# Moving shuffles, weight issues, sums, banks and late products in the first pair of an attention + MLP kernel

## The chip, the cores and the metric

The kernel runs on one core of one Trainium2 chip. The metric is device time in microseconds; lower is better. A profiled execution gives the trace that is quoted here. Engines are named as the profile names them: PE (TensorE), PEld (its weight loads), DVE (VectorE), ACT (ScalarE), POOL (GpSimd), SP (SyncE). A name such as L752 is line 752 of the kernel.

## The reference

Grouped-query attention (8 batches, 16 query heads, 4 key heads, 384 tokens, head size 64), followed by a residual MLP block over 1024 channels with a hidden width of 4096:

```
attn = softmax(q k^T / 8);  x = attn v          (8, 384, 1024)
a1  = alpha1 * x + beta1
tok = w_tok @ a1                                (mixes the 384 tokens)
u   = x + lam * tok
a2  = alpha2 * u + beta2
ch  = relu(a2 @ w_ch1) @ w_ch2                  (1024 -> 4096 -> 1024)
out = u + lam * ch
```

## The kernel before

**Stages.** The eight batches go in four pairs. An opening stage makes attention, token mixing and the turned a2 of batches 0 and 1 (`A` and `C` in the code). Then each pair runs a first product (a2 by w_ch1) and a second product (hidden by w_ch2); beside the second product of one pair, the attention of the next pair's two batches runs in small steps (`side`). Both products are done with seven block products in place of eight (a Strassen-like scheme), so there are sums and differences of operands, of weights and of results. The products are numbered 1 to 7; in the second product of the first pair the results of 2, 6, 7 and 4 are multiplied by lam and added to `out` by an accumulating DMA.

**Order.** The order of every engine's instructions is written by hand (`manual_schedule`): each engine runs its own instructions in the order of the code, and waits only for data, buffers and banks. In the opening stage a table `at` names for each of 36 turns (a quarter of a head pair's scores) what is emitted behind that turn's scores; a list behind it names the rest. In the products, a `yield` ends each segment of four matmuls (second product) and the table `plan` (`put(pair, phase, segment, ...)`) names what is emitted behind that segment.

**Names that the change touches.**

- `load_block(kind, gp)` (L553) issues from POOL the load of a quarter of the first product's weights, 512 KB in bf16, cast from float32; L1, L2, R1 and R2 are its four blocks, `gp` the pair of groups. With `home(c)` it goes to the arena, else to one of the six slots of the ring `w1`.
- `to_all(i, half, place)` (L1037) copies a row of 512 values to all partitions with a DVE shuffle; `to_all(2, ...)` makes alpha2, which `tok` needs (L334, on POOL in the opening stage).
- `tok(p)`: token mixing of a head pair on PE (L324, L328), its addition on DVE (L331), its product with alpha2 (L334). `turn(p)` turns the result on PE (L398), copied by ACT (L400); `C`'s first four are turned by DMA instead (L337). `av(p)`: probabilities by v on PE (L295), reciprocal and division on DVE (L300, L303). `a1(p)`: its product with g1 on DVE (L318, or L309 beside a second product).
- `diff_first(0, 4)` (L458) subtracts the turned a2 of both batches on DVE, an operand of product 7; `sums_first` (L454) makes another one.
- `share_banks(...)` opens the PSUM pools after the first product. `acc` has two banks for the accumulators of the second product, `sc0` to `sc2` two each for the attention. Ahead of it, Y (with product 4's sums, read by L702) had the banks 0 and 1, and X (read by L697) the banks 2 and 3.
- `second_product` has 21 turns of four segments: (product, third of the tokens) in the order 1, 2, 5 mixed, then 3, 6, 7 and 4, three each. Behind a turn ACT copies the bank (L764), and for products 6 and 7 DVE adds (L767); the result then stands in `later`. `flush(1)` takes one out of it twice a turn and emits `scaled`: the product with lam on POOL (L790) and the accumulating store from POOL (L442).
- `sum_w2`, `keep_w2`, `last_w2(c)`: differences of w_ch2 blocks on DVE (L499), stored by SP (L494); `last_w2` makes those of product 4 and frees a slot, and a free slot lets the queue issue its next load, here `load_w1` (L183, on POOL) for the next pair. `sum_w1` (L510, L515) makes sums of those for the next first product (L831; copied by L836).

The places of results are slices of one buffer; the next pair's first copies (L836) use the same buffer from s5 on:

```python
s2, s1, s5, s3 = ([snaps[:, (NST * i + ms) * 512:(NST * i + ms + 1) * 512] for ms in range(NST)] for i in range(4))
```

Of the kernel before, what the change touches and what calls it, by code (L numbers as in the profile page):

```python
# [13 lines left out]
def kernel(  # L14
# [27 lines left out]
    ADD = mybir.AluOpType.add  # L42
# [685 lines left out]
    def second_product(acc, later, flush, scaled):  # L728
# [17 lines left out]
        for k, (o, ms) in enumerate(turns):  # L746
            if (o, ms) not in xs_:
                begin(o, ms)
            x = xs_[o, ms]
            for t in range(NH):  # L750
                slot, rhs = raw[names[o], t // 4]
                nc.tensor.matmul(out=x, lhsT=lead_hid[:, t, FIRST2[o], ms * P:(ms + 1) * P],  # L752
                                 rhs=rhs[:, t % 4 * 512:(t % 4 + 1) * 512], start=(o in (1, 5) and t == 0), stop=(t == NH - 1),
                                 skip_group_check=True)
                if t % 4 == 3 and ms == NST - 1 and (o in (2, 3) or o == 4 and slot < RING):
                    free(slot)
                if t % 4 == 3 and t < NH - 1:
                    if t == 7 and turns[k + 1:] and turns[k + 1][0] in (3, 6, 7, 4):
                        begin(*turns[k + 1])
                    if t % 8 == 3 and later and later[0][1] != 4:  # L760
                        flush(1)
                    yield 1
            to = {1: s1, 2: s2, 5: s5, 3: s3, 6: s1, 7: s1, 4: s3}[o][ms]
            nc.scalar.copy(out=to, in_=x)  # L764
            if o in (6, 7):
                to = (s3 if o == 6 else s5)[ms]
                tt(out=to, in0=x, in1=to, op=ADD)  # L767
            if o in (2, 6, 7, 4):
                later.append((scaled, 1 if o == 2 else o, int(o in (7, 4)), ms, int(o in (6, 7)), to))
            yield 1  # L770

    def pair(i):
# [38 lines left out]

        if lead:
            yield from first_product(flush)
            share_banks("acc", "sc0", "sc1", "sc2")
            yield from second_product(pairs["acc"], later, flush, scaled)
            return

# [129 lines left out]
    with tc.manual_schedule(engines=order):  # L947
# [112 lines left out]
        scale_rows(1, nc.gpsimd)  # L1060
        split(1, 2, None, nc.gpsimd)
        load_v(1)
        for kind, gp in (("L1", 3), ("L2", 3), ("R1", 3), ("R2", 3), ("L1", 2), ("L2", 2)):
            load_block(kind, gp)

        def spill_all(b):
            nc.sync.dma_start(out=by_tok(out[b]), in_=xs[b])
# [30 lines left out]
        for c in range(4):  # L1098
            put(0, 0, (50, 72, 74, 44)[c], load_w2, "11", c)
            put(0, 0, (6, 14, 42, 46)[c], cast_w2, "21", c)  # L1100
            put(0, 1, (41, 43, 45, 47)[c], keep_w2, 1, c)
            put(0, 1, 38 + 2 * c, keep_w2, 3, c)
            put(0, 1, (9, 10, 13, 15)[c], sum_w2, 5, c)
            put(0, 1, (20, 21, 25, 26)[c], sums_first_hid, 2, c)
            put(0, 1, (28, 30, 31, 34)[c], sums_first_hid, 4, c)
            put(0, 1, (37, 40, 41, 43)[c], sum_w2, 6, c)
            put(0, 1, (44, 45, 49, 50)[c], sums_first_hid, 3, c)
            put(0, 1, (51, 54, 57, 58)[c], sum_w2, 7, c)
            put(0, 1, (60, 62, 64, 66)[c], last_w2, c)
# [29 lines left out]
        def product(n=1):  # L1139
            for _ in range(n):  # L1140
# [7 lines left out]
        A.q_transpose(1, 1, "tp")  # L1148
        at = {0: [(warmup, 3), (scale_rows, 0), (split, 0, 1, 0)], 1: [(A.k_transpose, 1, 1)],
              2: [(A.q_transpose, 2, 2, "av"), (split, 0, 1, 1)], 3: [(warmup, 1)],  # L1150
              4: [(A.av, 0)], 5: [(A.spread, lower, "tp"), (A.a1, 0)], 6: [(A.av, 1), (A.k_transpose, 2, 2, "tp"), (to_all, 2, 0, 0)],
              7: [(A.q_transpose, 4, 2, "av"), (A.a1, 1)], 8: [(A.av, 2), (to_all, 2, 1, 1), (flip_k, 1)],
              9: [(A.wtok_transpose, 0, "av"), (A.wtok_transpose, 1, "tp"), (flip_q, 1, 0, 4)],
              10: [(A.wtok_transpose, 2, "av"), (A.q_transpose, 6, 2, "mm"), (fill_h, 0)], 11: [(A.av, 3), (A.rows_r, "tp")],
              12: [(A.spread, upper, "av", "ACT"), (A.a1, 2), (fill_h, 4), (flip_q, 1, 4, 4)],
              13: [(A.tok, 0), (A.av, 4), (A.a1, 3)],
              14: [(A.tok, 1), (A.a1, 4)], 15: [(A.av, 5), (A.tok, 2), (A.a1, 5), (A.turn, 0, "tp")], 16: [(A.tok, 3), (A.turn, 1, "av")],
              17: [(A.av, 6), (A.a1, 6), (A.turn, 2, "tp")],
              18: [(A.tok, 4), (A.turn, 3, "av")], 19: [(A.av, 7), (A.a1, 7)], 20: [(A.tok, 5), (A.turn, 4, "tp")], 21: [(A.tok, 6)],
# [12 lines left out]
        for f, *a in ((C.turn, 4, "sc"), (C.av, 7), (early1, 10), (C.a1, 7), (early1, 11), (C.tok, 6), (C.turn, 5, "sc"), (early2, 10),  # L1172
                      (C.tok, 7), (early2, 11), (sums_first, 0, 2), (C.turn, 6, "sc"), (product, 2), (sums_first, 2, 1),
                      (C.turn, 7, "sc"), (sums_first, 3, 1), (spill_all, 1)):
            f(*a)
# [38 lines left out]
```

## Time and profile before

| | |
|---|---|
| median of 3 runs | 735.61 us (735.04 to 736.73) |
| profiled execution | 734.31 us |
| its span | 732.5 us |
| PE busy | 714.0 us (97%) |
| DVE busy | 542.6 us (74%) |
| ACT busy | 373.4 us (51%) |
| POOL busy | 200.6 us (27%) |
| granted TensorE clock | 1.00 |

The opening stage takes the first 60 us, the first pair's first product lasts until 130 us, its second product until 236 us. Rows of the profile's answers stand below. A row of the timeline has start, length (us), engine, line, operation, out<-in, shapes, count, and in brackets how long the engine stood idle before it and what ended that. A row of the waits has who waited for whom, the sum in us, how many times, the longest. A row of the DMA view has out<-in, the issuing queue, count, KB each and the us from issue to landing.

### The profile page before, as it was taken

What the parts mean: (1) busy time and instruction counts of PE and PEld (TensorE: products, weight loads), DVE (VectorE), ACT (ScalarE), POOL (GpSimd) and SP (SyncE); (2) the same over time, 40 slices, a digit from 0 to 9 for tenths busy, and PEclk for the clock granted to TensorE, in tenths of its full rate; (3) what the DMA queues carried; (4) which work ended last, traced back from release to release, by engine and by line L of the source; (5) the groups of instructions that cost most, each with busy time, mean ns of one, the idle gap of its engine ahead of it and who ended that gap; (6) DMA issues with size and microseconds to landing.
All of it is one profiled execution on the core that took longest, in us unless ns stands there. A gap on an engine that the chain in (4) does not pass through costs nothing.

```text
span 732.5 us, 14451 instructions
## 1 busy us (share of the span) xinstructions
PE 714.0 (97%) x5657; PEld 408.5 (56%) x5716; DVE 542.6 (74%) x1009; ACT 373.4 (51%) x566; POOL 200.6 (27%) x242
## 2 busy tenths in 40 slices
PE   8998999999999999999999999999999999999998
PEld 4665555455545566555555566655555566654444
DVE  8788876577897798649778988748958988762354
ACT  7877766545554666653433366663343366650000
POOL 8844243231073552201022344100002222000011
PEclk9999999999999999999999999999999999999999
DMA  9999999999999999979989999998999999937965
GB/s 166 184 236 205 192 188 225 228 250 211 366 309 251 182 184 200 208 232 218 261 193 205 179 162 195 210 221 211 276 227 178 212 126 145 169 123 261 304 173 102
DMA packets 197616, 153.26 MB, mean 209 GB/s; under 512 B 90540, under 2 KB 175892, under 8 KB 197292
## 3 DMA queue, kind: packets, MB, share of 16 engines
q0 software_dynamic: 109872, 64.47, 65.3%
q1 hardware_dynamic: 86988, 87.42, 43.4%
q8 instruction: 44, 0.72, 0.4%
q10 hardware_dynamic: 688, 0.46, 0.2%
q14 instruction: 24, 0.20, 0.1%
HBM read 155.23 MB, written 39.85 MB: 266 GB/s over the span
## 4 chain that ended last, share of the span: by engine, by line
PE 82%; DVE 9%; issue 3%; POOL 2%; DMA 2%; ACT 1%; DVEq 0%; POOLq 0%; ACTq 0%
PE C L897 28%; PE X L831 17%; PE Y L831 8%; PE C L752 6%; PE Z L831 4%; PE sc L260 4%; PE X L681 4%; PE sc L295 3%; PE Y L681 3%; PE sc L324 3%; DMA ops<-obuf 1%; DMA w<-in_moe_w_ch_dram 1%; DVE pad L565 1%; PE tok L324 1%; POOL w L553 1%
## 5 line engine op out<-in xcount | busy, mean ns | idle before, releaser
L897 PE MATMUL C<-w,arena 128*128 128x512 bf16 (+2 forms) x711 | 163.7, 373 | 1.6 <-issue 0.3
L269 ACT ACTIVATE es<-sc 128x1024 bf16<-128x1024 f32 x108 | 104.1, 1024 | 116.8 <-PE sc L260 106.8
L897 PEld LDWEIGHTS <-arena 128*128 128x128 bf16 x1040 | 94.7, 98 | 100.6 <-issue 5.0
L442 POOL DMA_DIRECT2D out_dram<-hT x45 | 39.9, 888 | 294.5 <-DVE hT L790 135.9
L836 ACT ACTIVATE hT<-X,bias 128x384 f32<-128x384 f32 x144 | 83.5, 580 | 60.0 <-PE X L831 55.3
L831 PEld LDWEIGHTS <-w 128*128 128x128 bf16 x768 | 75.0, 98 | 50.7 <-DVE ops L850 0.8
L831 PEld LDWEIGHTS <-pad 128*128 128x128 bf16 x576 | 56.3, 98 | 37.3
L183 POOL DMA_DIRECT2D w<-in_moe_w_ch_dram x48 | 45.7, 1006 | 98.5 <-PE X L831 37.7
L831 PE MATMUL X<-ops,w 128*128 128x384 bf16 x384 | 70.3, 327 | 0.4 <-DVE ops L850 0.4
L831 PE MATMUL X<-ops,pad 128*128 128x384 bf16 x384 | 70.3, 326 | 0.0
L897 PE MATMUL C<-pad,arena 128*128 128x512 bf16 (+2 forms) x288 | 69.5, 374 | 0.4
L324 PEld LDWEIGHTS <-wtokT 128*128 128x128 bf16 x576 | 38.9, 98 | 15.7 <-issue 2.5
L752 PEld LDWEIGHTS <-arena 128*128 128x128 bf16 x336 | 29.8, 98 | 30.9 <-issue 3.5
L331 DVE TENSOR_TENSOR xr<-sc,xr 128x384 f32<-128x384 f32 x48 | 26.5, 553 | 27.2 <-PE sc L324 14.3
L752 PE MATMUL C<-w,arena 128*128 128x512 bf16 x159 | 39.9, 380 | 0.5
L260 PE MATMUL sc<-qT,kT 64*128 64x384 bf16 (+2 forms) x504 | 37.4, 272 | 2.6 <-DVE xr L303 0.9
L838 DVE TENSOR_TENSOR arena<-Y,hT 128x384 bf16<-128x384 f32 x48 | 26.4, 556 | 17.5 <-ACT hT L836 15.8
L295 PEld LDWEIGHTS <-es 128*128 128x128 bf16 x864 | 32.8, 97 | 11.3
L831 PE MATMUL Z<-ops,w 128*128 128x384 bf16 x192 | 39.1, 327 | 0.0
L831 PE MATMUL Y<-ops,w 128*128 128x384 bf16 x192 | 39.1, 327 | 0.0
L269 ACT ACTIVATE hT<-sc 128x1024 bf16<-128x1024 f32 x36 | 35.9, 1037 | 4.4 <-PE sc L260 4.3
L842 ACT ACTIVATE arena<-X,bias 128x384 bf16<-128x384 f32 x48 | 27.9, 581 | 18.4 <-PE X L831 16.7
(190 smaller groups left out, 1173.6 us busy)
## 6 DMA issues: line engine op xcount, KB each, us to landing
w<-w2s SPq DMA_DIRECT2D x67, 512.0 KB, 4.9
w<-in_moe_w_ch_dram POOLq DMA_DIRECT2D x65, 512.0 KB, 10.1
pad<-w2s SPq DMA_DIRECT2D x25, 512.0 KB, 6.5
out_dram<-hT POOLq DMA_DIRECT2D x45, 256.0 KB, 7.6
out_dram<-xr SPq DMA_DIRECT2D x48, 192.0 KB, 5.6
q_raw<-in_q_dram POOLq DMA_DIRECT2D x28, 192.0 KB, 9.4
w2s<-w SPq DMA_DIRECT2D x10, 512.0 KB, 8.5
arena<-in_moe_w_ch_dram POOLq DMA_DIRECT2D x8, 512.0 KB, 16.7
```

Source lines behind the costliest of these rows:

```text
L183: nc.gpsimd.dma_start(out=w1[:, w1_slots[c]], in_=w1src[:, :, c * CW * P:(c + 1) * CW * P])
L260: nc.tensor.matmul(out=sc[:, hh, k % 4:k % 4 + n], lhsT=kT_[r, 2 * p // G, BLK[hh][sk], :], rhs=qT_[r, p, st:st + n, :], start=True, stop= ...
L269: nc.scalar.activation(out=e, in_=sc, func=EXP, scale=scale_qk)
L295: nc.tensor.matmul(out=av[:, hh, sq, :], lhsT=ess[k // 4][:, m % 2, k % 4, :], rhs=vb[:, sk, hk, :], start=(sk == 0), stop=(sk == NST - 1))
L324: nc.tensor.matmul(out=ps[:, tt, :], lhsT=wtokT[:, st, tt * P:(tt + 1) * P], rhs=a1s[p][:, st, :], start=(st == 0), stop=(st == NST - 1 an ...
L442: nc.gpsimd.dma_start(out=by_tok(out[b])[:, ms, dw * 512:(dw + 1) * 512], in_=o, accum_op=ADD)
L681: nc.tensor.matmul(out=ps[:, :n], lhsT=tb[G, o][:, dt, e * P:(e + 1) * P], rhs=opb(FIRST1[o], n)[:, dt], start=(o in (1, 2, 7) and dt == 0 ...
L752: nc.tensor.matmul(out=x, lhsT=lead_hid[:, t, FIRST2[o], ms * P:(ms + 1) * P], rhs=rhs[:, t % 4 * 512:(t % 4 + 1) * 512], start=(o in (1, ...
L831: nc.tensor.matmul(out=ps, lhsT=tb[g, o][:, dt, e * P:(e + 1) * P], rhs=opb(LEFT1[o])[:, dt], start=(o in (1, 2, 7) and dt == 0), stop=(dt ...
L836: nc.scalar.activation(out=snap[o, e], in_=ps, func=IDENT, bias=hi if o == 5 else lo)
L842: nc.scalar.activation(out=hid[:, t, 4], in_=ps, func=RELU, bias=hi)
L897: nc.tensor.matmul(out=x, lhsT=hid[:, t, LEFT2[o], ms * P:(ms + 1) * P], rhs=rhs[:, t % 4 * 512 + c0:t % 4 * 512 + c1], start=((not last o ...
```

## The change

Six things, all in the first pair:

- Four of the six weight issues ahead of the opening stage's turns (R1 and R2 of pair 3, L1 and L2 of pair 2) go behind turns 13, 15, 17 and 19, and the two that were behind turns 16 and 17 go behind 21 and 23.
- The shuffles of alpha2 go from turns 6 and 8 to turns 10 and 13.
- `diff_first` goes from turn 35 to behind the last `a1`.
- `sc0` is opened ahead of `acc`, so that `acc` takes the banks 2 and 3 and `sc0` the banks 0 and 1.
- `last_w2` goes from segments 60, 62, 64 and 66 to 61, 64, 68 and 71.
- Results of products 6 and 7 are taken out of `later` only behind turn index 16, that is in the turns with index 17 to 20; the result of product 6 goes to s2 instead of s3, since product 4's copy goes to s3.

```diff
-                    if t % 8 == 3 and later and later[0][1] != 4:
+                    if t % 8 == 3 and later and (later[0][1] == 1 or k > 16 and later[0][1] != 4):
                         flush(1)
...
             if o in (6, 7):
-                to = (s3 if o == 6 else s5)[ms]
-                tt(out=to, in0=x, in1=to, op=ADD)
+                to, base = (s2[ms], s3[ms]) if o == 6 else (s5[ms], s5[ms])
+                tt(out=to, in0=x, in1=base, op=ADD)
...
-            share_banks("acc", "sc0", "sc1", "sc2")
+            share_banks("sc0", "acc", "sc1", "sc2")
...
-        for kind, gp in (("L1", 3), ("L2", 3), ("R1", 3), ("R2", 3), ("L1", 2), ("L2", 2)):
-            load_block(kind, gp)
+        for kind in ("L1", "L2"):
+            load_block(kind, 3)
...
-            put(0, 1, (60, 62, 64, 66)[c], last_w2, c)
+            put(0, 1, (61, 64, 68, 71)[c], last_w2, c)
...
-              ... 6: [(A.av, 1), (A.k_transpose, 2, 2, "tp"), (to_all, 2, 0, 0)],
-              ... 8: [(A.av, 2), (to_all, 2, 1, 1), (flip_k, 1)],
+              ... 6: [(A.av, 1), (A.k_transpose, 2, 2, "tp")],
+              ... 8: [(A.av, 2), (flip_k, 1)],
...
-              10: [(A.wtok_transpose, 2, "av"), (A.q_transpose, 6, 2, "mm"), (fill_h, 0)], ...
+              10: [(A.wtok_transpose, 2, "av"), (to_all, 2, 0, 0), (A.q_transpose, 6, 2, "mm"), (fill_h, 0)], ...
...
-              13: [(A.tok, 0), (A.av, 4), (A.a1, 3)],
+              13: [(A.tok, 0), (A.av, 4), (A.a1, 3), (to_all, 2, 1, 1)],
...
-              35: [(C.tok, 5), (C.av, 6), (C.a1, 6), (diff_first, 0, 4)]}
-        at[16].append((load_block, "R1", 2, home(3)))
-        at[17].append((load_block, "R2", 2, home(0)))
+              35: [(C.tok, 5), (C.av, 6), (C.a1, 6)]}
+        for i, a in ((13, ("R1", 3)), (15, ("R2", 3)), (17, ("L1", 2)), (19, ("L2", 2)), (21, ("R1", 2, home(3))), (23, ("R2", 2, home(0)))):
+            at[i].append((load_block, *a))
...
-        for f, *a in (... (C.av, 7), (early1, 10), (C.a1, 7), (early1, 11), (C.tok, 6), ...
+        for f, *a in (... (C.av, 7), (early1, 10), (C.a1, 7), (diff_first, 0, 4), (early1, 11), (C.tok, 6), ...
```

More of the change, by code (lines that the diff above doesn't have):

```diff
@@ L1150 @@
               2: [(A.q_transpose, 2, 2, "av"), (split, 0, 1, 1)], 3: [(warmup, 1)],
-              4: [(A.av, 0)], 5: [(A.spread, lower, "tp"), (A.a1, 0)], 6: [(A.av, 1), (A.k_transpose, 2, 2, "tp"), (to_all, 2, 0, 0)],
-              7: [(A.q_transpose, 4, 2, "av"), (A.a1, 1)], 8: [(A.av, 2), (to_all, 2, 1, 1), (flip_k, 1)],
+              4: [(A.av, 0)], 5: [(A.spread, lower, "tp"), (A.a1, 0)], 6: [(A.av, 1), (A.k_transpose, 2, 2, "tp")],
+              7: [(A.q_transpose, 4, 2, "av"), (A.a1, 1)], 8: [(A.av, 2), (flip_k, 1)],
               9: [(A.wtok_transpose, 0, "av"), (A.wtok_transpose, 1, "tp"), (flip_q, 1, 0, 4)],
-              10: [(A.wtok_transpose, 2, "av"), (A.q_transpose, 6, 2, "mm"), (fill_h, 0)], 11: [(A.av, 3), (A.rows_r, "tp")],
+              10: [(A.wtok_transpose, 2, "av"), (to_all, 2, 0, 0), (A.q_transpose, 6, 2, "mm"), (fill_h, 0)], 11: [(A.av, 3), (A.rows_r, "tp")],
               12: [(A.spread, upper, "av", "ACT"), (A.a1, 2), (fill_h, 4), (flip_q, 1, 4, 4)],
-              13: [(A.tok, 0), (A.av, 4), (A.a1, 3)],
+              13: [(A.tok, 0), (A.av, 4), (A.a1, 3), (to_all, 2, 1, 1)],
               14: [(A.tok, 1), (A.a1, 4)], 15: [(A.av, 5), (A.tok, 2), (A.a1, 5), (A.turn, 0, "tp")], 16: [(A.tok, 3), (A.turn, 1, "av")],
@@ L1171 @@
                 f(*a)
-        for f, *a in ((C.turn, 4, "sc"), (C.av, 7), (early1, 10), (C.a1, 7), (early1, 11), (C.tok, 6), (C.turn, 5, "sc"), (early2, 10),
+        for f, *a in ((C.turn, 4, "sc"), (C.av, 7), (early1, 10), (C.a1, 7), (diff_first, 0, 4), (early1, 11), (C.tok, 6), (C.turn, 5, "sc"), (early2, 10),
                       (C.tok, 7), (early2, 11), (sums_first, 0, 2), (C.turn, 6, "sc"), (product, 2), (sums_first, 2, 1),
```

## The prediction

> **What bounds the kernel now.** I read the page first, then the table of stretches, the waits of the two places that the diff touches, their timelines, and the landings of the DMAs that it moves.
>
> ```profile
> span 732.5 us, 14451 instructions
> PE 82%; DVE 9%; issue 3%; POOL 2%; DMA 2%; ACT 1%; DVEq 0%; POOLq 0%; ACTq 0%
> 210.00:215.00 5.00, 4.13 (x38) 1.97 (x35) 4.90 (x8) 3.40 (x5) 4.18 (x5) 1.00 1.16 266
> ```
>
> The second line is the page's chain by engine: TensorE carries 82% of it, at a granted clock of 1.00 in the third line. The diff takes no matmul away and adds none, so it can gain only where TensorE waits. The third line is one stretch of the second product of the first pair (columns: PE, PEld, DVE, ACT, POOL busy, clock, DMA share, GB/s): PE idles 0.87 of 5 us while DVE is busy 4.90. The waits name such places, first of the opening stage (8 to 66 us), then of the end of the second product (193 to 245 us):
>
> ```profile
> PE tp L398 <- POOL obuf L334: 1.2, 1, 1.2
> PE tok L324 <- DVE hT L318: 1.2, 1, 1.2
> PE tp L344 <- DVE wtokT L347: 0.9, 1, 0.9
> ...
> PE sc L260 <- DVE xr L303: 0.9, 1, 0.9
> PE sc L324 <- ACT es L269: 0.6, 1, 0.6
> DVE pad L515 <- DMA w<-in_moe_w_ch_dram: 4.1, 1, 4.1
> ```
>
> The diff aims at the first, second and fourth of these, and at one more wait at 130 us. The time of the profiled execution is 734.31 us (span 732.5); the median of the three runs is 735.61, 1.30 above. I make the sum against 734.31 and add the same difference to the median.
>
> **Part 1: weight issues and shuffles.** POOL is the queue to look at. Timeline rows (start, length):
>
> ```profile
> 13.41 0.73 DVE L1037 STREAM_SHUFFLE vecs<-obuf 128x512 f32<-128x512 f32 x1
> 20.22 4.48 POOL L553 DMA_DIRECT2D w<-in_moe_w_ch_dram  x6
> 21.48 0.54 DVE L331 TENSOR_TENSOR arena<-tok,arena 128x384 f32<-128x384 f32 x1
> 24.64 4.28 POOL L334 TENSOR_TENSOR obuf<-arena,vecs 128x384 bf16<-128x384 f32 x4
> 25.07 0.55 DVE L331 TENSOR_TENSOR arena<-tok,arena 128x384 f32<-128x384 f32 x1
> 25.79 0.34 PE L398 MATMUL tp<-ident,obuf 128*128 128x128 bf16 x3 [1.24 <-POOL obuf L334]
> 27.26 0.56 DVE L331 TENSOR_TENSOR arena<-tok,arena 128x384 f32<-128x384 f32 x1 [1.11 <-PE tok L328]
> ```
>
> The first block of tokens is added at 22.02 (21.48 + 0.54), but its product with alpha2 stands on POOL behind six weight issues that end at 24.70, and PE's transpose waits 1.24 us for it. With two issues in front (2 x 4.48/6 = 1.5 us), POOL is free at 21.7 and the product ends at about 23.1 (4.28/4 = 1.07 each), before PE asks for it at 24.55. The wait goes. What is late next is DVE. Both shuffles (0.73 each) leave the places at 13.4 and 15.7, where the first stands before the qT copy and the second before the wtokT copy (PE's 0.9 us wait), but they come back at about 17 and 22.7 us, and DVE has nearly no idle time there. So the add at 25.07 comes between 0.0 and 0.5 us later, and the next add, which waited 1.11 us at 27.26 for PE, runs at 26.2 to 26.7. Gain 0.5 to 1.1 us; I take 0.9, near the wait of 1.24, since PE and ACT (whose copy stood behind the same transpose) run back to back afterwards.
>
> The four moved issues and the two that were at turns 16 and 17 come to stand between the eight POOL products of this batch: 6 x 0.75 + 8 x 1.07 = 13 us of POOL's time in some 14 us of turns 13 to 23. That is tight, but no more than POOL did from 20.22 on before. Do the weights come later? The DMA view gives the time to landing of the first and of the sixth load:
>
> ```profile
> w<-in_moe_w_ch_dram POOLq DMA_DIRECT2D x1, 512.0 KB, 8.5
> w<-in_moe_w_ch_dram POOLq DMA_DIRECT2D x1, 512.0 KB, 20.5
> ```
>
> The first was issued at 20.2 and lands at 28.7, the sixth was issued at 24.0 and lands at 44.5: one every 3.2 us, so they queue. The third's turn comes at 32, the fourth's at 35, the fifth's at 38; they will be issued at about 23, 26.5 and 29. Every landing stays as it is and this part costs nothing there. If the queue were empty, the fourth would land 3 us later, still ahead of its first use at 44.7.
>
> **Part 2: the difference of the operands.**
>
> ```profile
> 48.09 7.84 DMA ops<-obuf
> 54.34 0.73 DVE L318 TENSOR_TENSOR hT<-arena,vecs 128x384 bf16<-128x384 f32 x1
> 56.01 0.96 DVE L458 TENSOR_TENSOR ops<-ops 128x1536 bf16<-128x1536 bf16 x1 [0.94 <-DMA ops<-obuf]
> 57.71 0.56 DVE L318 TENSOR_TENSOR hT<-arena,vecs 128x384 bf16<-128x384 f32 x1
> 58.32 0.34 PE L324 MATMUL tok<-hT,wtokT 128*128 128x128 bf16 x3 [1.23 <-DVE hT L318]
> 62.64 2.49 PE L681 MATMUL X<-ops,pad 128*128 128x384 bf16 x13 [0.56 <-DVE ops L454]
> ```
>
> `diff_first` (L458) waits 0.94 us for a DMA transpose that ends at 55.94 (the first row, of the chain), and behind it on DVE stand the last head pair's reciprocal, division and product with g1 (L318 at 57.71), for which PE waits 1.23 us. Moved behind them, those three end at 55.07 + 0.2 + 0.56 + 0.56 = 56.4 instead of 58.27; `diff_first` then takes 56.4 to 57.4 and the adds behind it start 0.8 us earlier than at 58.2. PE gains 1.2, DVE 0.8 us up to the first product at 62.64. If the transpose does not come earlier by what part 1 gains, `diff_first` still waits until 55.97, and parts 1 and 2 together bring 1.2 us. Both parts: 0.8 to 2.3, taken 1.8.
>
> **Part 3: the banks.**
>
> ```profile
> 127.73 0.58 ACT L697 ACTIVATE arena<-X,bias 128x384 bf16<-128x384 f32 x1
> 128.99 1.13 DVE L702 SCALAR_TENSOR_TENSOR arena<-Y,bias,hT 128x384 bf16<-128x384 f32 x2
> 130.18 1.02 PE L752 MATMUL C<-arena 128*128 128x512 bf16 x3 [0.72 <-DVE arena L702]
> ```
>
> The second product's accumulators take the banks of Y, which DVE reads until 130.12. With `sc0` opened first they take those of X, last read at 128.31, before PE's last Y matmul ends (130.18 - 0.72 = 129.46). The scores, which then stand on Y's banks, come after four C matmuls (0.86 us), at 130.3, when DVE is through. Gain 0.72 if that wait is for the bank, 0 if it is for the data that L702 writes; the four matmuls read another slot of the hidden tile, so I take 0.7.
>
> **Part 4: products with lam, and the last sums.**
>
> ```profile
> 201.57 1.29 POOL L790 TENSOR_TENSOR hT<-hT,vecs 128x512 f32<-128x512 f32 x1
> 204.02 1.78 DVE L309 TENSOR_TENSOR a<-xr,vecs 128x384 bf16<-128x384 f32 x1
> 211.86 2.10 POOL L183 DMA_DIRECT2D w<-in_moe_w_ch_dram  x2
> 213.21 0.56 DVE L309 TENSOR_TENSOR a<-xr,vecs 128x384 bf16<-128x384 f32 x1
> 214.46 2.17 POOL L790 TENSOR_TENSOR hT<-hT,vecs 128x512 f32<-128x512 f32 x1 [0.51 <-DVE hT L767]
> 216.97 1.21 DVE L499 TENSOR_TENSOR w<-w,pad 128x2048 bf16<-128x2048 bf16 x1
> 225.75 0.87 POOL L442 DMA_DIRECT2D out_dram<-hT  x1 [0.30 <-POOL hT L790]
> ```
>
> DVE is full from 200 to 219. The same product takes DVE 1.78 us beside POOL's product and 0.56 without it, and POOL's takes 1.29 or 2.17. The Trainium skill ("SBUF — State Buffer", Who interferes with whom) says why: a DVE operation with two SBUF inputs and a GpSimd operation that reads SBUF lock each other out for a whole instruction. The trace agrees (1.22 us lost beside a product of 1.29).
>
> The new condition holds the six products back in the code until turn 17, but POOL is in order and waits for data, not for turns: it starts the first one as soon as the second of the two weight issues in front (211.86, gated by the last sums on DVE) is out, at about 214. So only four of the six really move, and the last ends at 228 to 231 instead of 225.45. In the stretch 201 to 213, DVE loses two collisions less (1.2 + 0.7 us) and one last sum comes behind the token adds; that ends PE's 0.9 us wait for L303. Two more last sums (1.21 each, L499) go behind 219, where DVE had idle time. The 0.6 us for ACT stays. So PE reaches the end 0.9 us earlier.
>
> There it meets another bound:
>
> ```profile
> out_dram<-hT POOLq DMA_DIRECT2D x1, 256.0 KB, 12.3
> w<-in_moe_w_ch_dram POOLq DMA_DIRECT2D x1, 512.0 KB, 7.0
> 234.12 0.93 POOL L183 DMA_DIRECT2D w<-in_moe_w_ch_dram  x1 [7.51 <-PE sc L398]
> 239.26 1.18 ACT L836 ACTIVATE hT<-X,bias 128x384 f32<-128x384 f32 x2 [0.72 <-PE X L831]
> 241.23 0.69 DVE L515 TENSOR_TENSOR pad<-w 128x1024 bf16<-128x1024 bf16 x1 [4.05 <-DMA w<-in_moe_w_ch_dram]
> ```
>
> The last store, issued at 225.75, lands 12.3 us later at 238.05; the load issued at 234.12 lands at 241.1 behind it, DVE waits 4.05 us for it, and PE 0.4 us behind DVE. POOL's transfers from 201 to 241 are one queue, and the same bytes lie in it after the change. If the queue is the bound, the load lands at 241 again and PE's 0.9 us is waited away; if it is not, PE keeps it, and up to 0.4 more. I take 0.4 of 0 to 1.3. The Trainium skill ("DMA: Bandwidth & Descriptors", Queues, rings and completion order) has each DMA engine take turns between queues; by that, the moved stores of weight sums from SP would share time with this queue later than before. No run here shows that price.
>
> **Sum.** 1.8 + 0.7 + 0.4 = 2.9 us: 731.4 on the profiled execution's scale, **732.7 us** on the median's. All best ends: 2.3 + 0.7 + 1.3 = 4.3, so 731.3. All worst ends: 0.8, so 734.8.
>
> **Rivals.**
> *Late stores (slower).* The results of product 7 lie where the next pair's first copies are written: L836 at 239.26 overwrites the third one, 1.2 us after its store landed. If POOL's products all run at the slow 2.17 with 0.30 + 0.87 for the store (3.3 us each), the sixth store is issued at 214 + 6 x 3.3 - 0.9 = 233 and with 12.3 us lands at 245.3; ACT's copy, and PE, which adds onto the same bank, stop for 6 us. Parts 1 to 3 give 2.5 back: 3.5 us slower, 739.1. It decides once the sixth store is issued later than about 227, at 12.3 us to landing. Against it: the first products alone took 2.25 us apart (201.57 to 203.82), and the loads are now ahead of the stores, so that the stores' own wait in the queue is shorter. Chance 0.12.
> *The gains are eaten in the opening stage.* DVE's second shuffle in a full stretch costs its 0.7, the transpose comes no earlier, and nothing is won at the end: 0.4 + 0.7 = 1.1 gained, 734.5. For it speaks DVE's lack of idle time. Chance 0.15, inside the bound below.
> *The queue is no bound.* Part 4 brings 1.3: 3.8 gained, 731.8. Chance 0.2.
> *The products don't move.* Were POOL held by something else, part 4 would bring only the moved sums: forecast less 0.4, 733.1. It is in the range.
>
> **How the numbers follow.** Forecast 0.53, the rivals as given. A measurement here can tell 0.2%, 1.5 us, from no change. Faster by that: 0.53 + 0.2 + a little of the second rival, 0.76. Within it 0.12, slower 0.12. The range reaches a little under the best ends, 730.7, and over all worst ends of the forecast, 735.2; it leaves out the slow rival.
>
> **What would show it.** In the changed profile: no wait of L398 for POOL near 25 us; L324 at 57 us without L318's wait, and L458 after it; the first product's X about 1.8 us earlier than 62.64; C's first matmuls without a wait for L702; L303's wait near 213 gone; the first product with lam after the two weight issues. PE waiting for ACT's L836, or DVE longer than 4 us for L515, in the next pair's first 10 us would show part 4 turning around, and X not earlier than 62 us would show part 1 or 2 wrong.

## The result, and the profile after

The changed kernel takes 732.95 us (median of 13 runs, 731.43 to 735.05); the kernel before, on the same chip, 735.12 us (13 runs, 733.93 to 737.66). The ratio is 0.9958, 95% interval 0.994 to 0.9976; the quotient of the two medians, 0.9970, lies inside it. The forecast was 732.7 us. The profiled execution took 731.92 us with a span of 729.9, against 734.31 and 732.5. (In the last set of runs below, three executions at a mean granted clock of 0.949 to 0.993 count in the medians but not in the ratios; the profiled one of the changed kernel is among them, and its trace is not used.)

From the page of the changed kernel, its chain by engine; then a row of its table of stretches, from 205 to 215 us (PE, PEld, DVE, ACT, POOL busy, clock, DMA share, GB/s; before, PE was busy 4.13 of the 5 us from 210 to 215):

```profile
PE 90%; DVE 4%; POOL 2%; DMA 1%; issue 1%; ACT 1%; DVEq 0%; ACTq 0%; POOLq 0%
205.00:215.00 10.00, 10.00 (x106) 5.90 (x105) 8.74 (x13) 6.54 (x10) 3.65 (x4) 1.00 1.18 321
```

TensorE's share of the chain is 90% instead of 82%, and in the stretch that had held an idle 0.87 us it is busy throughout. The waits of the changed kernel at the two places, of the opening (8 to 66 us) and of the end of the second product (193 to 245 us):

```profile
PE tok L324 <- DVE arena L331: 1.0, 2, 0.8
...
PE tp L398 <- DVE obuf L334: 0.7, 1, 0.7
```

```profile
DVE pad L515 <- DMA w<-in_moe_w_ch_dram: 2.9, 1, 2.9
...
PE sc L324 <- DVE a L309: 0.9, 1, 0.9
```

PE's wait of 1.2 us for the first product of POOL (L398), the one of 1.2 us for L318 and the one of 0.9 us for L303 are gone. Three new ones stand there: for DVE's add (L331), for DVE's product with alpha2 (L334) near 58 us, and for DVE's product L309 near 225 us. The timeline of the changed kernel in the order of the forecast's parts:

```profile
23.05 0.72 DVE L1037 STREAM_SHUFFLE vecs<-obuf 128x512 f32<-128x512 f32 x1
24.25 0.33 PE L324 MATMUL tok<-hT,wtokT 128*128 128x128 bf16 x3 [0.78 <-DVE arena L331]
24.92 0.33 PE L398 MATMUL tp<-ident,obuf 128*128 128x128 bf16 x3
...
56.45 0.33 PE L324 MATMUL tok<-hT,wtokT 128*128 128x128 bf16 x3
56.51 0.96 DVE L458 TENSOR_TENSOR ops<-ops 128x1536 bf16<-128x1536 bf16 x1 [0.62 <-DMA ops<-obuf]
61.42 2.49 PE L681 MATMUL X<-ops,pad 128*128 128x384 bf16 x13 [0.47 <-DVE ops L454]
...
128.07 1.03 PE L752 MATMUL C<-arena 128*128 128x512 bf16 x4
...
211.92 0.88 POOL L183 DMA_DIRECT2D w<-in_moe_w_ch_dram  x1 [2.38 <-DVE pad L499]
212.82 1.28 POOL L790 TENSOR_TENSOR hT<-hT,vecs 128x512 f32<-128x512 f32 x1
220.24 1.55 POOL L790 TENSOR_TENSOR hT<-hT,vecs 128x512 f32<-128x512 f32 x1
220.87 2.02 DVE L499 TENSOR_TENSOR w<-w,pad 128x2048 bf16<-128x2048 bf16 x1
222.71 1.57 POOL L790 TENSOR_TENSOR hT<-hT,vecs 128x512 f32<-128x512 f32 x1
223.62 1.08 DVE L309 TENSOR_TENSOR a<-xr,vecs 128x384 bf16<-128x384 f32 x1
224.76 0.34 PE L324 MATMUL sc<-a,wtokT 128*128 128x128 bf16 x3 [0.95 <-DVE a L309]
227.05 0.87 POOL L442 DMA_DIRECT2D out_dram<-hT  x1 [0.30 <-POOL hT L790]
...
240.23 1.46 PE L831 MATMUL X<-ops,w 128*128 128x384 bf16 x8
```

Read as a ledger against the same rows of before: the first product's X starts 1.22 us earlier (62.64 to 61.42); from there to the first C of the second product 0.89 less (67.54 to 66.65); from C to the X of the next pair's first product near 240 us 0.51 less (112.67 to 112.16). Together 2.62 us, the whole difference of the spans (732.5 to 729.9). Before, the last of these rows was:

```profile
242.85 1.47 PE L831 MATMUL X<-ops,w 128*128 128x384 bf16 x8 [0.43 <-DVE ops L850]
```

### The profile page after: what moved, and what is told of

Its sections match the earlier page's. It is cut to its first block, busy times and chain, and to the rows that moved or that the text cites. A ratio compares the mean times of both kernels' runs of the same rounds, so it can differ in the third digit from the quotient of the medians.

```text
span 729.9 us, 14511 instructions
## 1 busy us (share of the span) xinstructions
PE 717.4 (98%) x5716; PEld 408.7 (56%) x5716; DVE 543.9 (75%) x1009; ACT 373.8 (51%) x566; POOL 199.2 (27%) x242
## 4 chain that ended last, share of the span: by engine, by line
PE 90%; DVE 4%; POOL 2%; DMA 1%; issue 1%; ACT 1%; DVEq 0%; ACTq 0%; POOLq 0%
PE C L897 30%; PE X L831 17%; PE C L752 10%; PE Y L831 9%; PE Z L831 4%; PE sc L260 4%; PE X L681 4%; PE sc L295 3%; PE sc L324 3%; PE Y L681 3%; DMA ops<-obuf 1%; DVE pad L565 1%; PE Z L681 1%; PE tok L324 1%; POOL obuf L334 0%
## 5 line engine op out<-in xcount | busy, mean ns | idle before, releaser
L897 PE MATMUL C<-w,arena 128*128 128x512 bf16 (+2 forms) x744 | 168.3, 372 | 0.0
L836 ACT ACTIVATE hT<-X,bias 128x384 f32<-128x384 f32 x144 | 83.6, 582 | 60.0 <-PE X L831 55.2
L324 PEld LDWEIGHTS <-wtokT 128*128 128x128 bf16 x576 | 39.0, 98 | 16.4 <-issue 3.4
L331 DVE TENSOR_TENSOR xr<-sc,xr 128x384 f32<-128x384 f32 x48 | 26.5, 553 | 25.6 <-PE sc L324 14.3
```

Of the source, the lines that this page charges most:

```text
L324: nc.tensor.matmul(out=ps[:, tt, :], lhsT=wtokT[:, st, tt * P:(tt + 1) * P], rhs=a1s[p][:, st, :], start=(st == 0), stop=(st == NST - 1 an ...
L836: nc.scalar.activation(out=snap[o, e], in_=ps, func=IDENT, bias=hi if o == 5 else lo)
L897: nc.tensor.matmul(out=x, lhsT=hid[:, t, LEFT2[o], ms * P:(ms + 1) * P], rhs=rhs[:, t % 4 * 512 + c0:t % 4 * 512 + c1], start=((not last o ...
```

## The experiments

Four theories were open. T1: the three gains belong to the parts as the prediction has them (opening, banks, end of the second product). T2: the end of the second product gives nothing, only the parts ahead of it do. T3: part 4 gives only with both of its halves (late products and later sums). T4: what one profile shows at the end is run-to-run spread. The first kernels undo or do one part alone.

**One part of the opening alone.** First the issues: the kernel before with only two loads in the batch and the rest in the turns.

```diff
-        for kind, gp in (("L1", 3), ("L2", 3), ("R1", 3), ("R2", 3), ("L1", 2), ("L2", 2)):
-            load_block(kind, gp)
+        for kind in ("L1", "L2"):
+            load_block(kind, 3)
...
+        for i, a in ((13, ("R1", 3)), (15, ("R2", 3)), (17, ("L1", 2)), (19, ("L2", 2)), (21, ("R1", 2, home(3))), (23, ("R2", 2, home(0)))):
+            at[i].append((load_block, *a))
```

> Only the six weight issues are moved; the shuffles stay at turns 6 and 8. Theory (POOL's queue held the first transpose): the wait of 1.24 us of L398 for POOL ends, the first L398 starts at 24.6 instead of 25.79, and R2's issue ahead of the fourth product with alpha2 costs 0.4 later, so the scores near 50 us start 0.8 earlier than before and the first X of thirteen (62.64 before) starts 0.8 earlier. Rival (DVE was the bound there, and the shuffles had to go first): L398 waits no longer for POOL, but the scores near 50 us are less than 0.3 earlier.

One execution: 738.58 us beside 736.98 of the kernel before. Timeline of this kernel, opening and second product:

```profile
24.59 0.33 PE L398 MATMUL tp<-ident,obuf 128*128 128x128 bf16 x3
55.86 0.96 DVE L458 TENSOR_TENSOR ops<-ops 128x1536 bf16<-128x1536 bf16 x1 [1.57 <-DMA ops<-obuf]
58.16 0.34 PE L324 MATMUL tok<-hT,wtokT 128*128 128x128 bf16 x3 [1.86 <-DVE hT L318]
62.49 2.49 PE L681 MATMUL X<-ops,pad 128*128 128x384 bf16 x13 [0.56 <-DVE ops L454]
...
206.38 1.23 DVE L499 TENSOR_TENSOR arena<-pad,arena 128x2048 bf16<-128x2048 bf16 x1 [2.39 <-DMA w2s<-arena]
210.04 1.23 DVE L499 TENSOR_TENSOR arena<-pad,arena 128x2048 bf16<-128x2048 bf16 x1 [2.43 <-DMA w2s<-arena]
211.32 1.02 PE L752 MATMUL C<-arena 128*128 128x512 bf16 x4 [1.13 <-DVE arena L499]
216.43 0.61 PE L260 MATMUL sc<-qT,kT 64*128 64x128 bf16 x4 [2.32 <-DVE xr L303]
```

PE's wait for POOL is gone at once (24.59 instead of 25.79), and the scores near 50 us start 0.78 us earlier (49.24 for 50.02), as the theory has it. But the first X starts only 0.15 us earlier than in the profile of before. The transpose's landing stayed, `diff_first` waits 1.57 instead of 0.94 us for it, and with `diff_first` still ahead of L318 PE waits 1.86 instead of 1.23. So most of what the issues win is waited away where part 2 has its place. The time was lost in the second product, whose code here is that of before: DVE waits 4.8 us for stores of weight blocks, and PE behind it; more on that below.

Then the shuffles alone (`to_all` of the two blocks moved from turns 6 and 8 to 10 and 13):

```diff
-              ... 6: [(A.av, 1), (A.k_transpose, 2, 2, "tp"), (to_all, 2, 0, 0)],
+              ... 6: [(A.av, 1), (A.k_transpose, 2, 2, "tp")],
-              ... 8: [(A.av, 2), (to_all, 2, 1, 1), (flip_k, 1)],
+              ... 8: [(A.av, 2), (flip_k, 1)],
-              10: [(A.wtok_transpose, 2, "av"), (A.q_transpose, 6, 2, "mm"), (fill_h, 0)], ...
+              10: [(A.wtok_transpose, 2, "av"), (to_all, 2, 0, 0), (A.q_transpose, 6, 2, "mm"), (fill_h, 0)], ...
-              13: [(A.tok, 0), (A.av, 4), (A.a1, 3)],
+              13: [(A.tok, 0), (A.av, 4), (A.a1, 3), (to_all, 2, 1, 1)],
```

> Only the two shuffles are moved. Theory: the scores of turns 9 to 13 start 0.5 to 1.0 earlier (the waits for qT and wtokT shrink), but the first L398 still waits for POOL's six issues until 25.6 to 25.8, so nothing is left of it at 26 us (0 to 0.15 earlier) and at the first X (62.64). Rival (the shuffles carry the gain of the opening stage): L398 at 25.3 or earlier and the first X 0.5 or more earlier.

One execution: 735.55 us. The wait for POOL is 0.96 us, and the first X starts at 63.20: no gain. And `diff_first` alone:

```diff
-              35: [(C.tok, 5), (C.av, 6), (C.a1, 6), (diff_first, 0, 4)]}
+              35: [(C.tok, 5), (C.av, 6), (C.a1, 6)]}
-        ... (early1, 10), (C.a1, 7), (early1, 11), ...
+        ... (early1, 10), (C.a1, 7), (diff_first, 0, 4), (early1, 11), ...
```

> Only diff_first is moved behind the last a1. Theory of the prediction: the 1.23 us wait at 58.32 ends, and the first X (62.64) starts 0.8 earlier. Rival (the transpose's landing at about 56 us is the bound and DVE's chain from it on is the path): L324 of the last tok starts 1.2 or more earlier, but L458 still starts at 56.0, and as the last head pair's three operations now lie ahead of it, the adds behind L458 start at 57.0 instead of 58.2: 1.1 to 1.2 earlier, since nothing of part 1 eats into it.

One execution: 733.54 us. The timeline of this kernel at the end of the opening:

```profile
56.75 0.95 DVE L458 TENSOR_TENSOR ops<-ops 128x1536 bf16<-128x1536 bf16 x1
57.40 0.33 PE L324 MATMUL tok<-hT,wtokT 128*128 128x128 bf16 x3
61.71 2.49 PE L681 MATMUL X<-ops,pad 128*128 128x384 bf16 x13 [0.53 <-DVE ops L454]
```

PE's wait for L318 is gone and `diff_first` waits for nothing. The first X starts 0.93 us earlier than in the profile of before, the larger half of the opening's 1.22.

How far can single profiles be trusted here? Four kernels of this study keep the opening of before (before itself and the kernels with only the banks, only the late products, only the sums): first X at 62.64, 62.78, 63.27, 63.40, mean 63.02. Four keep the changed one (the changed kernel, the two without late products, the one with product 6 at once): 61.42, 60.99, 60.95, 61.58, mean 61.24. No value of one group reaches the other; the difference of the means is **1.79 us**, where the two profiles of before and after alone show 1.22. Against the mean of 63.02, the issues alone give 0.53 us, the shuffles alone still nothing, and `diff_first` alone 1.31; each of these is a single profile, held against a group that spreads by 0.76.

The profiles of the old opening also show a collision that the prediction did not count. In three of the four profiles of the old opening the first transpose does not wait for POOL at all. There POOL's first two products with alpha2 run back to back beside DVE's L318, as here in the kernel with only the banks:

```profile
24.34 2.03 POOL L334 TENSOR_TENSOR obuf<-arena,vecs 128x384 bf16<-128x384 f32 x2
24.44 2.37 DVE L318 TENSOR_TENSOR hT<-arena,vecs 128x384 bf16<-128x384 f32 x1
27.55 0.34 PE L324 MATMUL tok<-hT,wtokT 128*128 128x128 bf16 x3 [1.40 <-DVE arena L303]
```

This L318 takes 1.97 to 2.37 us in the three (0.54 us without POOL's product beside it), and PE waits 1.27 to 1.40 us for the L303 behind it. In the four profiles of the changed opening, where issues stand between POOL's products, no L318 near there takes more than 1.00 us.

**The banks alone.**

```diff
-            share_banks("acc", "sc0", "sc1", "sc2")
+            share_banks("sc0", "acc", "sc1", "sc2")
```

> Only the order of the pools is changed. Theory (the 0.72 us at 130.18 is the bank's): C's first matmuls start at 129.45 without a wait for L702, the scores behind them don't wait either, and the X of the next pair (236.41 before) starts 0.6 to 0.9 earlier. Rival (the wait is for what L702 writes): C at 130.2, nothing changes.

One execution: 736.3 us beside 736.98. The timeline:

```profile
129.12 1.13 DVE L702 SCALAR_TENSOR_TENSOR arena<-Y,bias,hT 128x384 bf16<-128x384 f32 x2
129.42 1.03 PE L752 MATMUL C<-arena 128*128 128x512 bf16 x3
```

C starts while DVE is still in L702, without a wait. From the first X to C it takes 66.64 us here. The six kernels with the old order take 67.52 to 67.54, and the five profiles with the new order and no further change ahead of it 66.64 to 66.66. The wait was the bank's, not the data's, and the order is worth 0.89 us in all of these: the wait of 0.72, and 0.17 that was not separated further.

**Everything but the late products.**

```diff
-                    if t % 8 == 3 and later and (later[0][1] == 1 or k > 16 and later[0][1] != 4):
+                    if t % 8 == 3 and later and later[0][1] != 4:
...
-                to, base = (s2[ms], s3[ms]) if o == 6 else (s5[ms], s5[ms])
-                tt(out=to, in0=x, in1=base, op=ADD)
+                to = (s3 if o == 6 else s5)[ms]
+                tt(out=to, in0=x, in1=to, op=ADD)
```

> The changed kernel with the products with lam of 6 and 7 put back (flushed at once, product 6's result in s3); all other moves stay. Theory (late products trade one wait for another): DVE collides with POOL again between 200 and 210 us and PE waits up to 0.5 for L303 near 211, but L309 of the last but one head pair no longer collides, so the 0.95 us wait of L324 near 225 goes; the next pair's X starts within 0.5 of the changed kernel's 234.38, rather earlier. Rival (the late products carry part 4): X starts 0.7 or more later than 234.38, and the 0.9 us wait for L303 is back.

One execution: 734.34 us beside 736.63. The timeline:

```profile
211.03 0.39 PE L260 MATMUL sc<-qT,kT 64*128 64x128 bf16 x4 [1.09 <-DVE xr L303]
237.43 1.05 ACT L836 ACTIVATE hT<-X,bias 128x384 f32<-128x384 f32 x2 [0.79 <-DMA out_dram<-hT]
241.68 1.47 PE L831 MATMUL X<-ops,w 128*128 128x384 bf16 x8 [1.41 <-DVE ops L850]
```

The wait for L303 stays at 1.09 us although the last sums were moved, more than the 0.5 of the theory; the wait for L309 near 225 us is gone, and the next pair's X starts at 234.25 instead of 234.38. So the theory is right that one wait is traded for another. The wait that the prediction's slow rival has from late stores stands here, 0.79 us of ACT for a store, without late products.

**The late products alone**, and **the last sums alone**, each on the kernel before:

```diff
-                    if t % 8 == 3 and later and later[0][1] != 4:
+                    if t % 8 == 3 and later and (later[0][1] == 1 or k > 16 and later[0][1] != 4):
...
-                to = (s3 if o == 6 else s5)[ms]
-                tt(out=to, in0=x, in1=to, op=ADD)
+                to, base = (s2[ms], s3[ms]) if o == 6 else (s5[ms], s5[ms])
+                tt(out=to, in0=x, in1=base, op=ADD)
```

> The kernel before with the late products only; last sums stay at 60 to 66. Theory: POOL's first product starts at about 214, DVE no longer collides from 201 to 213, the 0.87 us wait for L303 (213.23) shrinks to below 0.4, and a new wait of 0.5 to 1.2 for L309 stands near 226: X of the next pair at 236.2 to 236.8 (236.41 before). Rival (the late products alone bring the gain of part 4): X at 235.6 or earlier.

```diff
-            put(0, 1, (60, 62, 64, 66)[c], last_w2, c)
+            put(0, 1, (61, 64, 68, 71)[c], last_w2, c)
```

> The kernel before with only the last sums moved to segments 61, 64, 68, 71. Theory: the wait for L303 near 213 falls to 0.3 or less because one sum comes behind the adds, and nothing new waits near 226, since the sums run in DVE's idle time: X of the next pair 0.5 to 0.9 earlier than 236.41. Rival (collisions with POOL cause the wait, not the sums): the wait stays at 0.6 or more and X is within 0.3.

One execution each: 737.32 and 734.89 us, beside 736.63. The timeline of the first, then of the second:

```profile
214.79 2.69 DVE L499 TENSOR_TENSOR w<-w,pad 128x2048 bf16<-128x2048 bf16 x1
221.79 0.61 PE L260 MATMUL sc<-qT,kT 64*128 64x128 bf16 x4 [1.92 <-DVE xr L303]
```

```profile
213.55 0.39 PE L260 MATMUL sc<-qT,kT 64*128 64x128 bf16 x4 [0.44 <-DVE xr L303]
243.44 1.47 PE L831 MATMUL X<-ops,w 128*128 128x384 bf16 x8 [0.65 <-DVE ops L850]
```

Late products without later sums run into those sums: one of 1.21 us takes 2.69, and PE waits 1.92 us behind it. Neither the theory nor its rival had that. The sums alone halve the wait at 213 (0.87 to 0.44), so neither theory nor rival has its size, and lose 0.22 more at 243 us. From C to the next pair's first X they take 105.84 us, less than before (106.23) and less than the changed kernel (106.31); to the X near 240 us it is 112.51, between before (112.67) and the changed kernel (112.16). So the late products alone do harm, and that both halves do more than the sums alone is not shown.

**Product 6 at once, product 7 late.**

```diff
-                    if t % 8 == 3 and later and (later[0][1] == 1 or k > 16 and later[0][1] != 4):
+                    if t % 8 == 3 and later and (later[0][1] in (1, 6) or k > 16 and later[0][1] != 4):
```

> The changed kernel, but product 6's results are multiplied at once and only product 7's late. Theory: POOL's last product is done near 221, before the last two L309 (223.6 and 225.4 in the changed kernel), so those take 0.56 and PE's 0.95 us wait near 225 goes; the wait for L303 does not come back, as DVE had 1.9 us idle between 200 and 213; X at 233.5 (234.38 in the changed kernel). Rival (DVE is full between 200 and 213 once the three products are back there): a wait of 0.5 or more for DVE near 211, X within 0.3 of 234.38.

One execution: 735.37 us beside 736.63. The 0.95 us wait near 225 us is gone, but the one for L303 is back:

```profile
211.43 0.39 PE L260 MATMUL sc<-qT,kT 64*128 64x128 bf16 x4 [1.02 <-DVE xr L303]
```

The rival had the wait right, though not the next pair's X, which is 0.58 us later than in the changed kernel instead of within 0.3: the two waits are collisions of POOL's products with DVE's work that move with the products.

**Is the end of the second product told apart by time?** The changed kernel unchanged, and the one without late products a second time, in five rounds on one chip (kernel before there: 735.69 us).

> The changed kernel once more, timed. 2 to 3.5 us faster than before. Its second product (from the first C to the next pair's first X, 106.3 us in its first profile) may come out up to 1.5 us longer, if DVE waits longer for the stores of weights (L499 for w2s), which lay between 0 and 4.8 us in the kernels so far without any edit near it.

> The changed kernel with the products with lam of 6 and 7 put back, timed. Theory (late products and late sums gain only together): 1 to 2 us slower than the changed kernel, and a wait of PE for L850 of 1 us or more in the next pair, as in its single look. Rival (that look was chance, the late products bring nothing): within 0.5 us of the changed kernel.

The changed kernel: 734.04 us, ratio 0.9965 (0.9938 to 0.9993). Without late products: 733.79 us, 0.9981 (0.9948 to 1.0014). They are not told apart, so the rival of the second expectation holds: the late products bring nothing that the time shows. Of the executions at a mean granted clock of 0.999 or more, ten and nine, the medians are 733.38 and 733.43 us. The profile of the kernel without late products, its second, shows the row that had 1.41 us of wait:

```profile
240.60 1.47 PE L831 MATMUL X<-ops,w 128*128 128x384 bf16 x8 [0.43 <-DVE ops L850]
```

From C to this X the same code took 114.04 us in the first profile and 112.99 in the second. That spread of 1.05 is twice the 0.51 by which before and after differ there.

**A better opening, and earlier stores of weight blocks.** The second shuffle stands in front of L331, for which PE waits 0.78 us in the changed kernel; so it goes one turn later, the fourth issue one turn later, and `diff_first` behind C.tok:

```diff
-              13: [(A.tok, 0), (A.av, 4), (A.a1, 3), (to_all, 2, 1, 1)],
-              14: [(A.tok, 1), (A.a1, 4)], ...
+              13: [(A.tok, 0), (A.av, 4), (A.a1, 3)],
+              14: [(A.tok, 1), (A.a1, 4), (to_all, 2, 1, 1)], ...
-        for i, a in ((13, ("R1", 3)), (15, ("R2", 3)), ...
+        for i, a in ((13, ("R1", 3)), (16, ("R2", 3)), ...
-        ... (C.a1, 7), (diff_first, 0, 4), (early1, 11), (C.tok, 6), (C.turn, 5, "sc"), ...
+        ... (C.a1, 7), (early1, 11), (C.tok, 6), (diff_first, 0, 4), (C.turn, 5, "sc"), ...
```

> The changed kernel with three corrections of the opening stage: the second shuffle behind turn 14 instead of 13, R2's issue behind turn 16 instead of 15, diff_first behind the last but one tok. Theory: PE's waits of 0.78 us (24.25), 0.2 to 0.4 (28.98) and 0.6 to 0.7 (58.66) go, and the first X of thirteen starts at 60.0 to 60.4 instead of 61.42; 1.0 us faster than the changed kernel. Rival (DVE's work is the bound of the opening stage, so a wait only moves): X at 61.2 or later, no difference in time.

In the same five rounds: 732.86 us, ratio 0.9972 (0.994 to 1.0004). The timeline:

```profile
60.37 2.49 PE L681 MATMUL X<-ops,pad 128*128 128x384 bf16 x13 [0.54 <-DVE ops L454]
225.20 0.34 PE L324 MATMUL sc<-a,wtokT 128*128 128x128 bf16 x3 [1.66 <-DVE a L309]
```

The first X starts 0.87 us ahead of the mean of the changed opening (61.24), earlier than in every other kernel. Part of it is given back on the way to C (67.01 us for 66.65), and more at 225 us, where the wait for L309 is 1.66 instead of 0.95. The time does not tell it apart from the changed kernel.

The last one issues, on top of this, the four stores of the weight blocks 11 forty segments earlier, so that the sums of product 7, which overwrite these blocks, need not wait for them:

```diff
-            put(0, 1, (41, 43, 45, 47)[c], keep_w2, 1, c)
+            put(0, 1, (1, 2, 4, 5)[c], keep_w2, 1, c)
```

> The corrections of e9_opening, and the four stores of the blocks 11 (keep_w2(1, c)) issued behind segments 1, 2, 4 and 5 of the second product instead of 41 to 47, when SP is idle. Theory (the landing of these stores, which DVE must wait for before it overwrites the blocks, is what differs from run to run in the second product): L499 waits no longer for w2s<-arena, first C to next X is 105.5 to 106.0, and the times spread less; 0.3 to 1 us faster than e9_opening. Rival (the stores take the queue's bandwidth from the loads of other blocks at 130 to 145 us): PE or DVE waits for DMA between 150 and 195 us, and the time is equal or longer.

736.43 us, ratio 1.0019 (0.9987 to 1.0051): by the medians 3.6 us slower than the kernel that it changes, though the intervals overlap a little. Two rows of its waits from 66 to 245 us that neither before, nor the changed kernel, nor the better opening has in that window, and what follows from the first:

```profile
DVE w L499 <- DMA w<-in_moe_w_ch_dram: 2.4, 2, 1.5
...
DVE pad L499 <- DMA pad<-in_moe_w_ch_dram: 1.5, 2, 0.8
```

```profile
148.66 1.37 DVE L499 TENSOR_TENSOR w<-w,arena 128x2048 bf16<-128x2048 bf16 x1 [1.50 <-DMA w<-in_moe_w_ch_dram]
150.78 0.39 PE L260 MATMUL sc<-qT,kT 64*128 64x128 bf16 x4 [2.40 <-DVE xr L303]
```

DVE's wait for `w2s<-arena` (2.5 us with the better opening) is gone, and other sums, those of product 5 near 150 us, now wait 3.9 us for weights; behind one of them PE waits 2.40 us where it had no wait. So the rival was right, if a little earlier than it had said: the wait changed its owner. The three loads into `pad` take 20.9 us (median) to landing instead of 13.6. The Trainium skill ("DMA: Bandwidth & Descriptors", Queues, rings and completion order) has each DMA engine take turns between its queues; loads that come later when stores on another queue are moved beside them fit that, but no run here shows it by itself.

From C to the end the move costs 1.4 us (604.7 for 603.3). The rest of the 3.6 goes along with the clock: only two of its twelve executions have a mean granted clock of 0.999 or more, and they take 734.34 and 734.49 us, where ten of the better opening have it, with a median of 732.73. Whether the move causes the lower clocks is open. In the profiled one, the clock is 0.68 from 30 to 40 us, in the opening, which has the same code in both kernels.

**What the second product's spread is.** Time from C to the next pair's first X, DVE's wait for stores of weight blocks (`DVE arena L499 <- DMA w2s<-arena`), and PE's wait for L303 between 212 and 217 us, in kernels that have the same code there (but for the banks of the third):

| kernel | C to next X, us | DVE for stores | PE for L303 |
|---|---|---|---|
| before | 106.23 | none | 0.87 |
| only `diff_first` | 106.24 | none | 0.88 |
| only the banks | 106.26 | none | 0.90 |
| only the shuffles | 107.18 | 1.6 | 1.82 |
| only the issues | 111.0 | 4.8 | 2.32 |

With the shuffles alone the 0.95 us more are PE's longer wait for L303. With the issues alone, PE waits 1.13, 0.20 and 2.32 us within about 6 us, 2.78 more than before, and right behind these waits the granted clock (third number from the end) falls:

```profile
216.00:218.00 2.00, 1.57 (x7) 0.57 (x8) 1.97 (x4) 0.86 (x1) 1.49 (x3) 0.51 1.08 296
218.00:220.00 2.00, 1.95 (x16) 1.38 (x15) 0.78 (x2) 0.65 (x2) 1.82 (x1) 0.63 1.07 319
```

That is worth about 1.7 us (an estimate: 2 us at 0.51 and 2 at 0.63), and both together are 4.5 of the 4.8 us. It happens twice more: behind PE's wait of 1.92 us with the late products alone (0.50 from 222 to 225 us), so that part of that kernel's loss is the clock's, and behind one of 2.95 us in the opening of the last kernel above. It did not happen behind the 2.40 us in that same kernel, nor behind any wait below 1.92 us; what decides it is open.

Why DVE waits longer for the stores is not settled either. With the issues alone, the first store of the kept weights is issued 3.4 us later on SP than in before, and a transpose ahead of it takes 8.44 us instead of 4.94:

```profile
168.20 8.44 SPq L174 DMA_TRANSPOSE qT<-q_raw  x1
184.46 0.53 SPq L494 DMA_DIRECT2D w2s<-w  x1
```

(Before: 4.94 us for the transpose at 167.58, and the store at 181.08.) It isn't shown that an earlier weight issue causes it: the changed kernel has the same issues, waits 1.1 us for such a store, and takes 106.31.

## Why the prediction was right

**The time.** Forecast 732.7 (on the scale of the profiled execution a gain of 2.9 us), measured 732.95 with 2.6 us between the spans and 2.17 between the medians. T1 holds for the opening and the banks. For the end of the second product no gain is shown: T2 and T4 are left, and no time speaks for T3. That the medians agree within 0.25 us is in part luck, since part 4 came out by another way and part 1 met a collision that was not counted.

**Part 1, issues and shuffles: right in size at its place, not on its own.** It was to win 0.5 to 1.1 us, taken 0.9; the first L398 is 0.87 earlier. The doubt about the second shuffle came true, one add earlier than counted: DVE starts it at 23.05, the add behind it (at 23.09 before) starts at 23.67, and PE waits 0.78 us for that at 24.25. POOL's fit was called tight, and it is: with an issue in front of the fourth product with alpha2, PE waits 0.21 us for POOL at 28.98. What the prediction did not say is that most of the gain depends on part 2; the issues alone leave 0.15 (0.53 against the mean of four profiles). Nor did it count that POOL's products, back to back behind the issues, stretch DVE's L318, which three of four profiles of the old opening show in place of the wait for POOL.

**Part 2, the difference of the operands: the condition was named, and it held in part.** PE's 1.23 us went as worked out (L324 at 56.45 without a wait). The transpose did not come earlier with the rest: L458 still waits 0.62 us and runs at 56.51, half a microsecond later than before. That is the branch "1.2 us together", and the one pair of profiles gives 1.22. Four profiles on either side give 1.79, where 1.8 was taken (in two of the four changed ones L458 waits for nothing). The term was well sized, but a single pair of profiles could not have shown it.

**Part 3, the banks: right, and 0.19 larger than taken** (0.89 for 0.7; the upper bound of 0.72 was too low). It is the only part whose value repeats to 0.02 us.

**Part 4: the sum came out (0.51 for 0.4), by another way.** The 0.87 us for L303 did go. The first late product starts at 212.82 behind the second weight issue, as worked out (about 214). But PE did not reach the end 0.9 us earlier: POOL's products at 220.24 and 222.71 stretch a moved sum on DVE to 2.02 us (1.21 alone) and L309 behind it, at 223.62, to 1.08 (0.56 alone), and PE waits 0.95 for that L309. The prediction counted the collisions that leave 201 to 213 and not the ones that arrive at 220 to 226. From C to the next pair's first X nothing is won (106.23 and 106.31); the 0.51 comes after it, where DVE waits 2.92 instead of 4.05 us for the load (L515) and PE's 0.43 behind it is gone. So the queue was no fixed bound. Whether that is the change's doing is open: the spread of the same code is 1.05 us there, and the timed runs do not tell the kernel with late products from the one without. One reading of a row was wrong without harm to the sum: the L309 of 1.78 us at 204.02 lost its 1.22 us beside the product of 1.55 us that starts at 203.82, not beside the one of 1.29, which ends at 202.86.

**The slow rival** (late stores, 739.1) had the issue of the sixth store at 233 and the turning point at about 227, at 12.3 us to landing. POOL's products ran at 1.28 to 1.74 us and never at 2.17, so the store was issued at 227.05. That alone would not have ruled the rival out: at 12.3 us to landing the store is there at 239.35, and ACT's copy comes earlier now, at 237.23 instead of 239.26. But the store landed sooner, as the prediction argued against this rival. The DMA view from 226 to 240 us of the changed kernel:

```profile
out_dram<-hT POOLq DMA_DIRECT2D x1, 256.0 KB, 7.5
```

At 7.5 us instead of 12.3 it lands at about 234.6, and no wait of L836 for a store shows in the changed kernel. That such a wait can come true is shown by the kernel without late products, where ACT does wait for a store in one of its two profiles. **Gains eaten in the opening** fell with the first X at 61.42.

## What to carry to other kernels

A wait that is removed at one place is worth what the next rendezvous lets through: here the earlier POOL gave 0.15 us (0.53 against the mean of several profiles) until the operation that waits for a DMA was moved behind the one for which TensorE waits. Moving work off a full stretch of VectorE moves its collisions with GpSimd too, so count those at the place of arrival; and measure a change of half a microsecond by an interval between two marks in several profiles (the banks: 0.89 in all of them), since one profile against one other cannot tell it from the spread. Look at the granted clock behind a long wait before the whole loss is put down to the wait.

## What the runs showed of the hardware

- A bf16 sum of 128x2048 that takes DVE 1.21 us took 2.02 us and 2.69 us beside products of POOL, and a 128x384 product 1.08 (at 223.62 us of the changed kernel) and 1.74 (at 225.44) instead of 0.56. The Trainium skill ("SBUF — State Buffer", Who interferes with whom) has the two engines lock each other out for a whole instruction; the 0.5 to 1.5 us that these lost beside products of 1.55 to 1.58 us agree.
- The same instructions from C to the next pair's first X took between 106.23 and 111.0 us in five profiles. The two that took longer than 106.3 are those with DVE waiting for stores (1.6 and 4.8 us); in the longest, the granted clock was also 0.51 and 0.63 for 2 us each.
- In three profiles the granted clock fell to about 0.5 for some microseconds right behind a wait of TensorE of 1.92, 2.32 and 2.95 us. Behind waits up to 1.86 us, and behind one of 2.40, it did not.
- The last of the six accumulating stores of 256 KB landed 7.5 us after its issue in the changed kernel, where the weight loads are issued ahead of the six, and 12.3 us after it in the kernel before, where two stand among them (one profile each).
